# A DRAM-to-DRAM copy of x cut into 512 pieces of 5 KB instead of 64 of 40 KB, in a fused attention and feed-forward kernel

## The chip, the cores and the metric

The kernel runs on one core of one Trainium2 chip. The metric is the device time of one execution in microseconds (us). KB in the tables are units of 1024 bytes.

## The reference

One transformer block on 2048 tokens of width 640, with multi-query attention (32 query heads of 20 channels, one key and one value head) and a dense layer with squared ReLU, both on the same normalized input. Cut to what matters:

```python
xn = _layernorm(x, axis=-1)            # x: [1, 2048, 640] bf16
# attention: q = xn@wq as [32 heads, 2048, 20]; k = xn@wk, v = xn@wv are [2048, 20]
scores = einsum("bhqd,bkd->bhqk", q, k) * 20 ** -0.5
attn = (softmax(scores) @ v, heads joined) @ wo
# dense: h = relu(xn@w1 + b1) ** 2, 1536 wide
ffn = h @ w2 + b2
return x + attn + ffn
```

## The kernel before

**Attention.** The 2048 queries are four chunks of 512, the 32 heads eight groups of four; each of these 32 blocks runs over 16 tiles of 128 keys. For each key tile TensorE (PE) writes four 128x512 score tiles into PSUM (`q:` and `d:` in the written order). Their exponentials are taken either by ScalarE (ACT, L1083) or, by an integer approximation in four terms, by VectorE (DVE, L1093 and L1107), GpSimd (POOL, L1106) and accumulating DMAs (L1130). PE then multiplies the results with v (`v:` and `u:`).

**Fillers.** Between the score tiles PE does the projections and the dense layer: the transposes `T`, the keys `KT`, the values `V`, the queries `Q1` and `QC`, the dense layer `FFN`, `FP` and `OUT`.

**Order.** Each engine's instructions stand in a list written out by hand (`ORDER`, from L67), one list for PE, DVE, ACT, POOL and for the sync engine's queue of DMAs (SP). An engine works through its list in order and waits at an instruction until what it depends on is there. Every large load has a semaphore of its own.

**Start of SP's list:** `X0 X2 wq0 X4 X6 X8 b2 X12 xb b1 w11 wq w10 w20 w22 w23 w13 QD2_2 ...`. `X0` to `X12` (L622) load the rows of x into SBUF. `wq0` loads the first 80 columns of the query weights, `wq` (L628) the other 560 columns, as 128 partitions of 5 rows. `b1`, `w1`.. and `w2`.. are the bias and the weights of the dense layer. `HOLD` (L60) lets some of these wait for an evacuated transpose: `xb` and `wq` for `TE2`, `w11` for `TE6`, `w10` for `TE4`.

**The copy of x.** `xb` (L647) copies x from the input to a tensor in DRAM of the same shape. `XA` (L648) then adds the bias b2 to every row of that tensor, by an accumulating DMA issued from POOL that waits for `b2` (L646, 16 copies of b2 in DRAM) and for `xb`. Later `XR` (L869) loads the sum by 128 rows of tokens, sixteen times, as the residual that is added to the output.

**Around XA in POOL's list:** `... PW11 XN11 PW12 XA PW13 PW14 XN14 PW15 XN15 LIB p:27.1 ...`. `PW` (L676) makes the reciprocal standard deviation of 128 rows, `XN` (L677) normalizes them (rows 13 on DVE, 14 and 15 on POOL), and `T13` to `T15` on PE transpose the result. `LIB` loads another POOL library.

**Around Q1 in PE's list:** `q:38,39 q:40,41 Q1 Q1 T12 Q1 T13 q:42,43 Q1 q:44,45 Q1 KT6 ...`. `Q1` (L773) makes the queries of the second block in five steps and waits for `wq` and `wq0`.

**Four other copies of DRAM to DRAM** (`wd0` to `wd3`, L641 to L644) move rows of wo in about 100 to 150 us from the start: `wd0` 96 rows in one run of the outer dimension, the other three as 4 groups of 20, 12 and 8 rows, with the 4 outermost:

```python
wd8 = wod[96:128, 0, :].rearrange("(j r) n -> j r n", r=8)             # L638, j = 4
hrows = lambda r: A_wo[r:r + HPG * DH, :].rearrange("(j r) n -> j r n", r=DH)
```

Of the small transfers, `drs<-OR` (L945) moves 4 rows of 2 KB from SBUF, `R<-drs` (L946) 128 rows of 64 bytes, and `qT<-QCr` (L800) mostly 20 rows of 1 KB.

Of the kernel before, what the change touches and what calls it, by code (L numbers as in the profile page):

```python
# [38 lines left out]
def _pl(z):  # L39
# [20 lines left out]
HOLD = dict(wq="TE2", b1="TE5", w1=("TE4", "TE6", "TE8", "TE10"), w2=("TE12", "TE13", "TE14", "TE15"), wo=("RL3_2", "RL3_4"), wd="RL3_7",  # L60
            fr=[f"OUT{16 + k}.16" for k in range(4)])
# [433 lines left out]
def bass_parallel_sum__grouped_kv_mqa__dense_activation_squared_relu__prompt_kernel(nc, A_x, A_wq, A_wk, A_wv, A_wo, B_x, B_w1, B_b1, B_w2, B_b2, out):  # L495
    es = ExitStack()
    with es:
# [71 lines left out]
        xb = nc.dram_tensor("xb", [S, D], BF16, kind="Internal").ap()  # L569
# [14 lines left out]
        def one():  # L584
            nsem[0] += 1
            return newctr(f"d{nsem[0]}")
# [3 lines left out]
        def op(name, eng, fn, deps=(), **kw):  # L590
            o = Op(name, eng, fn if isinstance(fn, list) else [fn], deps, **kw)
            assert name not in made, name
            made[name] = o
            return o

        def load(name, eng, fn, deps=()):
            return op(name, eng, fn, deps, dma=one())
# [46 lines left out]
            lambda e: e.dma_start(wd32[:, DH:32, 1, :], hrows(wr0)[:, 8:DH, :])))]  # L644
        op("texp", "ACT", lambda e: e.preload_act_table_set("natural_log_exp_and_others"))
        l_b2 = load("b2", "SP", lambda e: e.dma_start(b2r[0].rearrange("(a n) -> a n", a=ST), B_b2.rearrange("(o n) -> o n", o=1).to_broadcast([ST, D])))  # L646
        l_xb = load("xb", "SP", lambda e: e.dma_start(xb.rearrange("(p a) d -> p (a d)", p=128), A_x[0].rearrange("(p a) d -> p (a d)", p=128)), [HOLD["wq"]])  # L647
        xa_op = op("XA", "POOL", lambda e: e.dma_start(xb.rearrange("(p a) d -> p (a d)", p=128).rearrange("p (k n) -> p k n", k=5),  # L648
                                                       b2r.rearrange("o (k n) -> o k n", k=5).to_broadcast([128, 5, 2048]), accum_op=ALU.add, max_dma_last_dim=4096), [l_b2, l_xb], dma=one())

# [379 lines left out]
        for e in ENG:  # L1030
            nth = {}
            for word in ORDER[e].split():
                w, _, ns = word.partition("@")
                ns = [int(x) for x in ns.split(",")] if ns else []
                k, _, a = w.partition(":")
# [64 lines left out]
        for u, x in sets.items():  # L1100
            assert sorted(x.order) == list(range(HPG))
            for j in range(1, NTERM):
                w = f"{u}.{j}"
                if ("p", w) in plan:
                    e, ns = plan["p", w]
# [3 lines left out]
                elif ("j", w) in plan:  # L1109
                    e, ns = plan["j", w]  # L1110
# [210 lines left out]
```

## Time and profile before

| | |
|---|---|
| median of 3 runs | 663.84 us (662.64 to 665.05) |
| profiled execution, its own time | 664.51 us |
| its span in the trace | 662.7 us |
| PE busy | 654.4 us, 99% of the span |
| ACT busy | 649.7 us, 98% |
| DVE busy | 625.3 us, 94% |
| POOL busy | 536.7 us, 81% |

The span is the stretch of the trace in which the engines work; the profiled execution's own time is 1.8 us longer. Times in the trace count from the start of the span. A line of a group names source line, engine, operation, output and inputs, count, busy time and the mean of one. "SPq" is the sync engine's queue, its durations are those of issuing a DMA and not of the transfer; how long a transfer took stands in the table of issues ("us to landing").

### The profile page before, as it was taken

The page shows a single profiled execution, that of the slowest core. Times are in us where ns is not written, and L with a number is a line of the kernel's source. Part 1 is how long each engine was busy: PE and PEld are TensorE (multiplying, and loading weights), DVE is VectorE, ACT ScalarE, POOL GpSimd, SP SyncE. Part 2 cuts the span into 40 slices and gives each one's busy share as a digit, 9 for nine tenths or more (in the row PEclk, how much of TensorE's full clock was granted, in tenths as well). Part 3 has the DMA queues.
Part 4 walks back from the last instruction along what each step waited for, and adds up shares of the span by engine and source line. Part 5 has one row for each costly group of instructions (what it writes and reads, how often), then busy time and mean ns, then how long its engine had stood idle before and what let it go on. Part 6 is the DMA issues. An engine that isn't in the chain of part 4 may idle for free.

```text
span 662.7 us, 22005 instructions
## 1 busy us (share of the span) xinstructions
PE 654.4 (99%) x9422; PEld 216.9 (33%) x9422; DVE 625.3 (94%) x1123; ACT 649.7 (98%) x716; POOL 536.7 (81%) x532
## 2 busy tenths in 40 slices
PE   8999999999999999999999999999999999999998
PEld 4432222333322223333332222333333322223444
DVE  8879999999999999999999999999999999999997
ACT  7999999999999999999999999999999999999996
POOL 1729899899898889898999989888999988899400
PEclk9999999999999999999999999999999999999999
DMA  8794857888897995696957645798888654858732
GB/s 293 187 245 96 185 110 163 166 183 187 185 186 161 183 182 120 129 184 125 178 107 155 122 92 99 151 189 170 158 174 165 132 121 91 178 105 177 141 110 71
DMA packets 53814, 102.06 MB, mean 154 GB/s; under 512 B 15948, under 2 KB 31452, under 8 KB 53652
## 3 DMA queue, kind: packets, MB, share of 16 engines
q0 software_dynamic: 18544, 68.17, 55.4%
q1 hardware_dynamic: 34308, 31.94, 16.8%
q8 instruction: 74, 1.21, 0.8%
q10 hardware_dynamic: 864, 0.54, 0.3%
q14 instruction: 24, 0.20, 0.1%
HBM read 23.26 MB, written 10.01 MB: 50 GB/s over the span
## 4 chain that ended last, share of the span: by engine, by line
PE 58%; ACT 34%; DMA 3%; DVE 3%; SPq 1%; issue 0%; POOL 0%
PE ps L600 57%; ACT PT L1083 34%; DVE tx L1093 1%; DMA tx<-tx 1%; DMA cmore<-drs 1%; DMA tx<-in_A_x_dram 1%; PE ps L1005 1%; SPq L800 0%; SPq L969 0%; SPq L963 0%; DVE xnT L694 0%; SPq L622 0%; DVE OR L662 0%; PE ps L700 0%; PE ps L703 0%
## 5 line engine op out<-in xcount | busy, mean ns | idle before, releaser
L1083 ACT ACTIVATE PT<-ps 128x1024 bf16<-128x1024 f32 (+1 forms) x693 | 640.4, 1089 | 2.3 <-PE ps L600 1.9
L1093 DVE TENSOR_SCALAR tx<-ps 128x512 uint16<-128x512 f32 x656 | 424.8, 683 | 21.8 <-PE ps L600 15.1
L1106 POOL INT64_ADD tx<-tx x375 | 396.3, 1132 | 54.3 <-DVE big L836 15.2
L600 PE MATMUL ps<-qT,kT 20*128 20x512 bf16 x2048 | 265.4, 384 | 3.3 <-ACT PT L1083 1.2
L600 PEld LDWEIGHTS ps<-qT,kT 20*128 20x128 bf16 x2048 | 69.0, 91 | 248.7 <-ACT PT L1083 132.4
L600 PE MATMUL ps<-PT,vx 128*32 128x512 bf16 x1392 | 131.7, 383 | 0.0
L1130 POOL DMA_DIRECT2D tx<-tx x118 | 121.3, 1028 | 10.3 <-POOL tx L1106 7.8
L600 PE MATMUL ps<-tx,vxs 128*32 128x512 bf16 x1220 | 115.4, 384 | 0.0
L600 PE MATMUL ps<-tx,vx 128*32 128x512 bf16 x864 | 81.3, 384 | 0.5 <-DMA tx<-tx 0.5
L600 PE MATMUL ps<-w_sb,big 128*32 128x320 bf16 x1536 | 79.1, 302 | 0.0
L600 PE MATMUL ps<-xnT,w_sb 128*32 128x512 bf16 x960 | 78.0, 383 | 0.0
L1107 DVE TENSOR_SCALAR tx<-tx 128x2048 uint16<-128x2048 uint16 x89 | 61.2, 700 | 0.6 <-PE ps L600 0.2
L600 PEld LDWEIGHTS ps<-PT,vx 128*32 128x32 bf16 x1392 | 34.6, 95 | 39.1 <-issue 31.1
L600 PEld LDWEIGHTS ps<-w_sb,big 128*32 128x32 bf16 x1536 | 33.8, 95 | 30.2 <-issue 20.0
L600 PEld LDWEIGHTS ps<-tx,vxs 128*32 128x32 bf16 x1220 | 30.0, 94 | 36.1 <-issue 27.1
L828 DVE TENSOR_SCALAR hT_tmp<-ps,b1col 128x512 bf16<-128x512 f32 x48 | 35.7, 744 | 0.8 <-PE ps L600 0.6
L600 PE MATMUL ps<-xnT,wq_sb 128*32 128x512 bf16 (+2 forms) x480 | 35.5, 357 | 0.0
L600 PEld LDWEIGHTS ps<-tx,vx 128*32 128x32 bf16 x864 | 21.4, 94 | 26.2 <-issue 21.5
L600 PEld LDWEIGHTS ps<-xnT,w_sb 128*32 128x32 bf16 x960 | 19.9, 95 | 28.8 <-issue 19.3
L600 PE MATMUL ps<-wo_c,OC 128*32 128x320 bf16 x496 | 28.0, 301 | 0.0
L1112 POOL INT64_ADD tx<-tx x14 | 26.9, 1924 | 0.9 <-DVE big L836 0.5
L944 DVE COPY OR<-ps 128x512 f32<-128x512 f32 x30 | 20.4, 680 | 1.7 <-PE ps L600 1.6
(87 smaller groups left out, 221.5 us busy)
## 6 DMA issues: line engine op xcount, KB each, us to landing
tx<-tx POOLq DMA_DIRECT2D x111, 512.0 KB, 5.9
tx<-tx POOLq DMA_DIRECT2D x7, 1024.0 KB, 8.8
w_sb<-in_B_w_dram SPq DMA_DIRECT2D x8, 480.0 KB, 9.6
big<-OR SPq DMA_DIRECT2D x71, 40.0 KB
xb<-in_A_x_dram SPq DMA_DIRECT2D x1, 2560.0 KB, 11.1
xb<-b2r POOLq DMA_DIRECT2D x1, 2560.0 KB, 19.8
xr<-xb SPq DMA_DIRECT2D x16, 160.0 KB, 3.2
out_dram<-out_sb SPq DMA_DIRECT2D x14, 160.0 KB, 3.6
```

The source lines that it names most:

```text
L600: return lambda e: e.matmul(out_(), l, val(r), start=val(start), stop=val(stop), tile_position=tp, skip_group_check=loose)
L828: o = evac(ref, f"RL{qc}_{f}", "DVE", lambda e: e.tensor_scalar(out=hT_tmp[:, k % 2, :], in0=ps[:, ref.n, :], scalar1=b1col[:, f:f + 1], s ...
L944: tn = evac(pv_ref[b], f"TN{b}", "DVE", lambda e: e.tensor_copy(out=OR[:, a, :], in_=acc()), or_users[a])
L1005: parts = [lambda e, l=l, r=r, first=first, last=last: e.matmul(ps[:, at(ref), 0:HW], l, r, start=first, stop=last, skip_group_check=k < N ...
L1083: o = op(f"a:{a}", e, lambda e, qk=qk, slots=slots: e.activation(out=some(PT, slots), in_=some(ps, [r.n for r in qk.takes]), func=AF.Exp, ...
L1093: o = op(f"e:{a}", e, lambda e, x=x, i=i, n=n, refs=refs: e.tensor_scalar(out=x.ref(0)[:, i * 512:(i + n) * 512].bitcast(U16) if n == 1 el ...
L1106: fn = dict(POOL=lambda e, x=x, j=j: e.int64_add(out=x.ref(j).bitcast(I64), in0=x.ref(0).bitcast(I64), in1=TSTEP * j * 0x0001000100010001) ...
L1107: DVE=lambda e, x=x, j=j: e.tensor_scalar(out=x.ref(j).bitcast(U16), in0=x.ref(0).bitcast(U16), scalar1=TSTEP * j, scalar2=None, op0=ALU.a ...
L1112: o = op(f"j:{w}", e, lambda e, x=x: e.int64_add(out=two(*sorted((x.at[2], x.at[3]))).bitcast(I64), in0=two(*sorted((x.at[0], x.at[1]))).b ...
L1130: fn = (lambda e, x=x: e.dma_start(*reversed(sums_of(x.at)), accum_op=ALU.add)) if k == "b" else (lambda e, x=x, p=pairs[0]: e.dma_start(x ...
```

## The change

The walk over x in the copy `xb` is written differently on both sides. Before, partition-like index p (128) was outermost and its 16 rows of 640 elements followed: all of it is one contiguous run, which went out as 64 pieces of 40 KB. After, each of the 128 stretches of 16 rows is cut into g = 4 parts of 4 rows (2560 elements, 5 KB), and g is put outermost: first the first parts of all 128 stretches, then the second parts, and so on. Same bytes, same places, same semaphore, same position in SP's list.

```diff
@@ -644,7 +644,7 @@
-        l_xb = load("xb", "SP", lambda e: e.dma_start(xb.rearrange("(p a) d -> p (a d)", p=128), A_x[0].rearrange("(p a) d -> p (a d)", p=128)), [HOLD["wq"]])
+        l_xb = load("xb", "SP", lambda e: e.dma_start(xb.rearrange("(p g a) d -> g p (a d)", p=128, g=4), A_x[0].rearrange("(p g a) d -> g p (a d)", p=128, g=4)), [HOLD["wq"]])
         xa_op = op("XA", "POOL", lambda e: e.dma_start(xb.rearrange("(p a) d -> p (a d)", p=128).rearrange("p (k n) -> p k n", k=5),
                                                        b2r.rearrange("o (k n) -> o k n", k=5).to_broadcast([128, 5, 2048]), accum_op=ALU.add, max_dma_last_dim=4096), [l_b2, l_xb], dma=one())
```

## The prediction

> **What bounds the kernel now.** I read the busy shares first, then the chain that ended last, then the first 60 us by engine, since the copy is issued at 9.8 us.
>
> ```profile
> PE 654.4 (99%) x9422; PEld 216.9 (33%) x9422; DVE 625.3 (94%) x1123; ACT 649.7 (98%) x716; POOL 536.7 (81%) x532
> PE 58%; ACT 34%; DMA 3%; DVE 3%; SPq 1%; issue 0%; POOL 0%
> ```
>
> The chain is PE for 58% and ACT for 34%: with both busy for 98 to 99% of the span, a stop of PE early on is never worked off. The copy itself is not in the chain. So the question is who waits for it, for what stands behind it in the queue, and with how much room. The timeline of the SP queue shows that neighbourhood (start, duration, line):
>
> ```profile
> 4.69 0.58 SPq L622 DMA_DIRECT2D tx<-in_A_x_dram  x1
> 9.80 0.50 SPq L647 DMA_DIRECT2D xb<-in_A_x_dram  x1
> 16.06 0.40 SPq L631 DMA_DIRECT2D b1row<-in_B_b_dram  x1
> 19.09 0.60 SPq L630 DMA_DIRECT2D w_sb<-in_B_w_dram  x1
> 19.73 0.64 SPq L628 DMA_DIRECT2D wq_sb<-in_A_wq_dram  x1
> 52.99 0.42 SPq L869 DMA_DIRECT2D xr<-xb  x1
> ```
>
> The table of issues gives their sizes and the us from issue to landing:
>
> ```profile
> xb<-in_A_x_dram SPq DMA_DIRECT2D x1, 2560.0 KB, 11.1
> xb<-b2r POOLq DMA_DIRECT2D x1, 2560.0 KB, 19.8
> wq_sb<-in_A_wq_dram SPq DMA_DIRECT2D x1, 700.0 KB, 5.7
> w_sb<-in_B_w_dram SPq DMA_DIRECT2D x8, 480.0 KB, 9.6
> b2r<-in_B_b_dram SPq DMA_DIRECT2D x1, 20.0 KB, 6.4
> wod<-in_A_wo_dram SPq DMA_DIRECT2D x1, 120.0 KB, 2.4
> wod<-in_A_wo_dram SPq DMA_DIRECT2D x1, 100.0 KB
> wod<-in_A_wo_dram SPq DMA_DIRECT2D x1, 60.0 KB
> wod<-in_A_wo_dram SPq DMA_DIRECT2D x1, 40.0 KB
> R<-drs SPq DMA_DIRECT2D x30, 8.0 KB, 4.1
> drs<-OR SPq DMA_DIRECT2D x30, 8.0 KB
> qT<-QCr SPq DMA_DIRECT2D x105, 20.0 KB
> ```
>
> The copy lands at 9.80 + 11.1 = 20.9 us, wq at 19.73 + 5.7 = 25.4. Who needs them, from the timelines of POOL, DVE and PE:
>
> ```profile
> 25.96 1.82 POOL L648 DMA_DIRECT2D xb<-b2r  x1
> 27.99 0.56 POOL L676 TENSOR_TENSOR rstd<-mv,nhalf 128x1 f32<-128x1 f32 x1 [0.21 <-DVE mv L667]
> 32.04 0.88 POOL L677 TENSOR_SCALAR big<-tx,mv,rstd 128x640 bf16<-128x640 bf16 x1
> 42.22 1.03 POOL L1106 INT64_ADD tx<-tx  x1 [9.31 <-DVE vxs L733]
> ...
> 29.00 0.75 DVE L677 TENSOR_SCALAR big<-tx,mv,rstd 128x640 bf16<-128x640 bf16 x2
> ...
> 29.29 0.61 PE L600 MATMUL ps<-xnT,wq_sb 128*20 128x512 bf16 x8
> 30.56 0.47 PE L700 MATMUL ps<-ident,big 128*128 128x128 bf16 x5
> 34.00 0.79 PE L700 MATMUL ps<-ident,big 128*128 128x128 bf16 x10
> 41.26 0.83 PE L600 MATMUL ps<-xnT,wq_sb 128*32 128x512 bf16 x12
> ```
>
> POOL reaches XA at 25.96, 5.0 us after the copy landed; PE reaches Q1 at 29.29, 3.9 us after wq landed. That is all the room there is.
>
> **The change: which engines carry it.** Sixteen DMA engines share a transfer. The profile prints a landing only where it finds sixteen increments for each issue. Beside the program, the rows above sort by the count of the outermost dimension: 64 (xb), 96 (wod, 120 KB), 128 (R, wq) and 16 (b2r) have a landing; 4 (the other three wod copies, drs<-OR) and 20 (qT) have none. So the outermost dimension is what is shared out, and one of 4 entries can occupy four engines at most. The new walk has g = 4 outermost on both sides: 2560 KB on four engines, 640 KB each, instead of 160 KB on sixteen. The size of a piece then matters little; the engines do. The three small wod copies are this very form, DRAM to DRAM.
>
> [...]
>
> **How long the copy takes.** DMA share and GB/s, the last two columns, while the copy runs on sixteen engines:
>
> ```profile
> 12.00:14.00 2.00, 1.57 (x41) 0.71 (x29) 2.00 (x10) 1.74 (x2) 1.13 (x2) 1.00 0.93 369
> 12.00:18.00 6.00, 5.08 (x94) 2.44 (x83) 5.45 (x22) 5.74 (x5) 3.11 (x5) 1.00 0.99 343
> 16.00:18.00 2.00, 1.75 (x35) 0.79 (x34) 1.71 (x7) 2.00 (x3) 0.91 (x2) 1.00 1.08 332
> ```
>
> A busy engine moves 369 / (16 x 0.93) = 24.8 GB/s at best, 343 / (16 x 0.99) = 21.7 over the six us, 332 / (16 x 1.08) = 19.2 at the end. I take 24.8: four engines ask DRAM for a quarter of that traffic, so the least disturbed row is the nearest. 655,360 B at 24.8 GB/s is 26.4 us (30.2 and 34.1 by the others). For what is fixed I take the 2.4 us of the 120 KB copy, which moves only 7.5 KB per engine. New landing: 9.80 + 2.4 + 26.4 = 38.6 us, 17.7 later.
>
> [...]
>
> **What that moves.** Issuing: 512 pieces instead of 64; the load at 4.69, also 512 pieces, took 0.58 against 0.50 us, and SP is free until 16.06. Nothing.
>
> POOL: XA waits from 25.96 to 38.6, and behind it in the list PW13, PW14, XN14, PW15, XN15 and LIB: +12.6. XN13 on DVE needs PW13: 38.6 + 2.0 (25.96 to 27.99) + 0.6 + about 0.5 = 41.7 instead of 29.75; T13 stood at 30.56. XN15 ended at 32.9, its transpose is in the group at 34.00: 1.1 us of room and more.
>
> SP's queue: it works in order; b2r, 20 KB issued behind the loads of x, took 6.4 us where 120 KB alone took 2.4. On the four engines b1, w11 (480 KB) and wq (700 KB) stand behind the copy; these last two spread over sixteen, so their share of 30 and 43.75 KB per engine comes after it: 1.2 + 1.8 us at 24.8 GB/s. wq lands at 38.6 + 3.0 = 41.6. PE stops at Q1 from 29.29 to 41.6: **+12.3 us**. T13, due at 30.56 + 12.3 = 42.9, finds XN13 done (41.7), so the two stops lie over each other and wq ends last. ACT has a few score tiles left and then stands too.
>
> Later users: b1 is needed just before 41.26, landed by 39; w10 lands 1.2 after wq. XA lands at 38.6 + 19.8 = 58.4, before the first XR (52.99 + 12.3 = 65.3). The first accumulation of POOL at 42.22 had waited 9.31 for DVE, so LIB fits. None adds.
>
> **The restart.** PE was busy nearly without a break from 29 us on, and would now pause for 12. Two rows show the same dummy matmul at the start and later:
>
> ```profile
> 2.57 4.60 PE L1041 MATMUL ps<-hT_tmp,OR 128*128 128x512 bf16 x13
> 12.44 0.59 PE L1041 MATMUL ps<-hT_tmp,OR 128*128 128x512 bf16 x2
> ...
> 30.00:40.00 10.00, 9.80 (x159) 4.50 (x157) 6.48 (x18) 9.93 (x12) 2.70 (x4) 1.00 1.05 210
> ```
>
> Two take 0.59 us, 0.21 apart and 0.38 for the last; thirteen at that pace are 2.9 us, at the start they took 4.60: 1.7 us lost, although the granted clock reads 1.00. No row shows a pause in the middle, so 0 to 1.7; I take 1.2, nearer to the start, which is the only row of a PE that had stood still. Against it stands that DVE, POOL and the loads catch up during the stop: at 30 to 40 us PE lacked 0.2 us, so I take off 0.3 (0 to 0.5).
>
> [...]
>
> **The sum.** 12.3 + 1.2 - 0.3 = +13.2 us. The profiled execution took 664.51 (span 662.7 and 1.8 around it), so it would be 677.7; it lies 0.7 over the median of 663.84, so the forecast for the median is 677.0, 2.0% slower. By bounds of the terms: 24.8 GB/s without restart and with 0.5 off, +11.8 (675.6); at 19.2 GB/s the copy is 7.7 longer and the two shares behind it take 3.9 instead of 3.0, so with 1.7 for the restart +22.6 (686.4).
>
> **The rivals.**
> - *Not slower: the copy stays on sixteen engines*, because the walk is put back into one run or shared out by the 128. It then lands near 21 us, before 25.96, and the time is 663.8. It decides at 13.8 us of transfer (25.96 - 9.80 - 2.4), which eight engines at 24.8 GB/s just reach (13.2). For it: the same bytes in the same places. Against: g stands outermost on both sides, with steps of 5 KB outside steps of 20 KB; only with the two loops exchanged would it be one run. 0.06.
> - *wq slips past the copy*, so that only XA's wait counts. T13 then moves from 30.56 to 41.7, +11.1, with the restart and what is caught up 675.8. Against: b2r's 6.4 us. 0.10.
> - *The four engines are slower*, as in the row 16 to 18, by traffic of their own: 680 to 686. The aggregate of 343 GB/s against 369 speaks for it, the quarter of the traffic against. 0.17.
> - *Fewer than four engines.* Two: 52.8 us, so 26.4 more, 703. 0.03.
> - *Faster*: smaller pieces let b1 and wq through sooner. wq already has 3.9 us of room, so it gives nothing unless it moves something I do not see. 0.01.
> - My forecast, 674 to 680: 0.63.
>
> **How the numbers follow.** About 0.3% (2 us) is what a measurement of this kernel can tell from no change. Slower: 0.63 + 0.10 + 0.17 + 0.03 = 0.93; same 0.06; faster 0.01. The range from 672.5 to 686 takes in the forecast, the second and most of the third rival, and at its lower end an engine faster than any row.
>
> **What the changed profile would show.** Landing of xb near 29 us instead of 11.1, or no landing at all in its row; XA on POOL at about 38.6; the first matmul of xnT and wq_sb with 512 columns at about 41.6, and behind it the DMA share near a quarter (0.25, some 100 GB/s) from 26 us on; from there everything moved by 12 to 14 us to the end. Wrong would be: XA still at 26, wq landing before the copy, or a stop that ACT and PE make up for by the end.

## The result, and the profile after

| | before | after |
|---|---|---|
| median of 5 runs each | 663.99 us (662.64 to 665.05) | 680.59 us (678.78 to 681.29) |
| ratio | | 1.0243, 95% interval 1.0221 to 1.0265 |
| profiled execution, its span | 664.51, 662.7 us | 679.16, 677.3 us |
| mean granted clock in the profiled execution | 1.000 | 0.987 |

The change costs 16.6 us. Medians, here and below, are over all executions of a kernel; ratios are formed from undisturbed ones only, which makes a visible difference in `e7_both` and `e9_both_16`.

The page of the changed kernel: busy shares, the chain's shares, the costliest group of ACT and three DMA issues (KB, us to landing).

```profile
PE 657.7 (97%) x9422; PEld 217.4 (32%) x9422; DVE 625.6 (92%) x1123; ACT 649.8 (96%) x716; POOL 536.7 (79%) x532
...
PE 61%; ACT 32%; DMA 4%; DVE 2%; POOL 0%; issue 0%
...
L1083 ACT ACTIVATE PT<-ps 128x1024 bf16<-128x1024 f32 (+1 forms) x693 | 640.6, 1089 | 16.7 <-PE ps L600 16.4
...
xb<-in_A_x_dram SPq DMA_DIRECT2D x1, 2560.0 KB
xb<-b2r POOLq DMA_DIRECT2D x1, 2560.0 KB, 19.2
...
wq_sb<-in_A_wq_dram SPq DMA_DIRECT2D x1, 700.0 KB, 18.4
```

The row of ACT's exponentials before:

```profile
L1083 ACT ACTIVATE PT<-ps 128x1024 bf16<-128x1024 f32 (+1 forms) x693 | 640.4, 1089 | 2.3 <-PE ps L600 1.9
```

The work is the same (the same counts, ACT busy for 649.8 us against 649.7). What has grown is idle time, for ACT's exponentials from 2.3 to 16.7 us, and PE's busy time: the same 9422 matmuls take 657.7 us instead of 654.4. The copy's row has lost its landing, as the four-group copies of wo have none, and wq takes 18.4 us to land instead of 5.7. The chain that ended last now has the copy in it. Its stretch around that (start, duration, engine):

```profile
9.80 27.90 DMA xb<-in_A_x_dram
37.70 0.31 issue
38.01 1.82 POOL xb L648
39.83 0.63 POOL rstd L676
...
40.48 0.45 DVE big L677
...
41.19 1.03 PE ps L600 x8
```

The copy takes 27.90 us and releases XA at 38.01; PW13 and XN13 follow, and PE goes on with Q1 at 41.19 (the chain puts Q1 down to XN13; the experiments will show that it waited for wq). The timeline of PE has the stop itself, the last entry of a line being the idle time before it:

```profile
28.94 0.40 PE L600 MATMUL ps<-qT,kT 20*128 20x512 bf16 x4
41.19 1.03 PE L600 MATMUL ps<-xnT,wq_sb 128*20 128x512 bf16 x8 [11.85 <-DVE mv L670]
```

The same first step of Q1 stood at 29.29 and took 0.61; now it takes 1.03. Why is in the windows (us; busy time of PE, PEld, DVE, ACT, POOL; then granted clock, DMA share, GB/s):

```profile
12.00:18.00 6.00, 5.49 (x106) 2.70 (x99) 5.60 (x24) 6.00 (x6) 3.10 (x5) 1.00 0.26 101
28.00:30.00 2.00, 1.34 (x31) 0.59 (x27) 1.37 (x5) 2.00 (x3) 0.00 (x0) 1.00 0.26 110
30.00:34.00 4.00, 0.00 (x0) 0.00 (x0) 0.00 (x0) 1.31 (x2) 0.00 (x0) 0.75 0.72 238
34.00:38.00 4.00, 0.00 (x0) 0.00 (x0) 0.00 (x0) 0.00 (x0) 0.00 (x0) 0.50 0.58 191
42.00:46.00 4.00, 4.00 (x30) 1.46 (x30) 1.10 (x4) 1.28 (x2) 2.02 (x3) 0.50 1.06 209
...
32.00:33.00 1.00, 0.00 (x0) 0.00 (x0) 0.00 (x0) 0.00 (x0) 0.00 (x0) 0.51 1.04 389
48.00:49.00 1.00, 1.00 (x12) 0.11 (x4) 0.00 (x0) 0.91 (x1) 0.00 (x0) 0.50 0.99 194
49.00:50.00 1.00, 1.00 (x18) 0.69 (x14) 0.26 (x1) 0.67 (x1) 0.00 (x0) 0.95 0.97 206
```

While the copy runs alone the DMA share is 0.26, four engines of sixteen. All compute engines stand at 34 to 38. The granted clock falls to half at 32.0 and is whole again only at 49.1, 7.9 us after PE had resumed and although PE shows as busy throughout.

How much the rest of the program has moved is read from one late instruction whose place in the lists is fixed, the second load of wo_c (L635; the two start times end the line). Before, then after:

```profile
L635 SPq DMA_DIRECT2D wo_c<-in_A_wo_dram x2: 434/439/444, 77.4 to 106.6; - x2
```

```profile
L635 SPq DMA_DIRECT2D wo_c<-in_A_wo_dram x2: 434/439/444, 92.5 to 121.8; - x2
```

106.6 has become 121.8: a **shift** of 15.2 us. ACT's score instructions, compared one by one, show the same 15.2 from 35 us (by the clock of before) on to 535, and the spans differ by 14.6 at the end. So 11.9 us are the stop, about 3.3 the restart, and only 0.6 is made up later.

### The profile page after: what moved, and what is told of

Same layout as the page of the kernel before. It is cut to its first block, busy times and chain, and to the rows that moved or that the text cites. A ratio compares the mean times of both kernels' runs of the same rounds, so it can differ in the third digit from the quotient of the medians.

```text
span 677.3 us, 22005 instructions
## 1 busy us (share of the span) xinstructions
PE 657.7 (97%) x9422; PEld 217.4 (32%) x9422; DVE 625.6 (92%) x1123; ACT 649.8 (96%) x716; POOL 536.7 (79%) x532
## 4 chain that ended last, share of the span: by engine, by line
PE 61%; ACT 32%; DMA 4%; DVE 2%; POOL 0%; issue 0%
PE ps L600 60%; ACT PT L1083 32%; DMA xb<-in_A_x_dram 4%; DVE tx L1093 1%; PE ps L1005 1%; POOL xb L648 0%; PE ps L700 0%; ACT xnT L696 0%; DVE OR L662 0%; DVE OR L663 0%; DVE ident L613 0%; DVE PT L611 0%; DVE big L677 0%; ACT OC L657 0%; POOL rstd L676 0%
## 5 line engine op out<-in xcount | busy, mean ns | idle before, releaser
L1083 ACT ACTIVATE PT<-ps 128x1024 bf16<-128x1024 f32 (+1 forms) x693 | 640.6, 1089 | 16.7 <-PE ps L600 16.4
L1093 DVE TENSOR_SCALAR tx<-ps 128x512 uint16<-128x512 f32 x656 | 425.0, 684 | 21.3 <-PE ps L600 14.6
L600 PE MATMUL ps<-tx,vxs 128*32 128x512 bf16 x1220 | 115.4, 384 | 0.0
L600 PE MATMUL ps<-xnT,wq_sb 128*32 128x512 bf16 (+2 forms) x480 | 36.5, 366 | 12.1 <-DVE mv L670 11.8
L600 PEld LDWEIGHTS ps<-w_sb,big 128*32 128x32 bf16 x1536 | 33.8, 95 | 30.2 <-issue 20.0
## 6 DMA issues: line engine op xcount, KB each, us to landing
w_sb<-in_B_w_dram SPq DMA_DIRECT2D x8, 480.0 KB, 10.4
```

The lines of the kernel that those rows point to most:

```text
L600: return lambda e: e.matmul(out_(), l, val(r), start=val(start), stop=val(stop), tile_position=tp, skip_group_check=loose)
L1083: o = op(f"a:{a}", e, lambda e, qk=qk, slots=slots: e.activation(out=some(PT, slots), in_=some(ps, [r.n for r in qk.takes]), func=AF.Exp, ...
L1093: o = op(f"e:{a}", e, lambda e, x=x, i=i, n=n, refs=refs: e.tensor_scalar(out=x.ref(0)[:, i * 512:(i + n) * 512].bitcast(U16) if n == 1 el ...
```

## The experiments

The theory: the copy runs on as many engines as its outermost dimension has entries, here four; XA and wq wait for it; PE stops, and restarts at half clock. The main rival at this point: the 512 smaller pieces themselves are slow. All edits are to the changed kernel unless said.

**Many small pieces on sixteen engines** (`e1_g16`).

```diff
-"(p g a) d -> g p (a d)", p=128, g=4
+"(p g a) d -> g p (a d)", p=32, g=16
```

> 512 pieces of 5 KB as in the change, in the same kind of order, but with g = 16 outermost instead of 4 (32 stretches of 64 rows, cut in 16). My theory (the four entries of the outermost dimension confine the copy to four engines): the copy lands near 21 us again, POOL reaches XA at 26.0 and PE reaches Q1 at 29.3 without waiting; time 664, within 2 us of the kernel before. Rival (the small pieces or the strided order make the copy slow): the copy lands near 38 and the time is 679 to 681.

Median 663.38 us, ratio 1.0004 (0.9982 to 1.0026). The copy lands after 12.2 us; from its window, POOL's and PE's timelines:

```profile
12.00:18.00 6.00, 5.42 (x109) 2.73 (x98) 5.67 (x24) 6.00 (x5) 3.11 (x5) 1.00 0.98 293
```

```profile
25.80 1.82 POOL L648 DMA_DIRECT2D xb<-b2r  x1
```

512 pieces of 5 KB, sixteen outermost: DMA share 0.98, XA does not wait, and the time is that of before. The copy lands 1.1 us later than before (12.2 against 11.1), within its 5.0 us of room; to the kernel the size of the pieces costs nothing here.

**Few large pieces on four engines** (`e2_g4_big`): `p=16, g=4` on both sides, 64 pieces of 40 KB as before the change, but g = 4 outermost.

> The other way round: 64 pieces of 40 KB as before, but with g = 4 outermost (16 stretches of 128 rows, cut in 4). My theory: four engines again, the copy lands near 37 to 39 us, time 679 to 682 as with the change. Rival (the size of the pieces): the copy lands near 21 and the time is 664.

Median 680.05 us, ratio 1.0247 (1.0230 to 1.0264): the whole loss, with the pieces of before.

```profile
12.00:18.00 6.00, 5.49 (x84) 2.79 (x75) 5.59 (x25) 6.00 (x6) 3.12 (x5) 1.00 0.21 86
```

```profile
40.98 1.04 PE L600 MATMUL ps<-xnT,wq_sb 128*20 128x512 bf16 x8 [12.17 <-DVE mv L670]
```

With the run above this decides between engines and pieces: the engines.

**Eight engines** (`e3_g8`): `p=64, g=8`.

> 512 pieces of 5 KB with g = 8 outermost. My theory: eight engines, 320 KB each; in the changed kernel an engine moved about 24.5 GB/s, so 13.4 us and some 2 fixed: landing at 25.0 to 25.6, just before POOL reaches XA (25.96); wq behind it lands about 3 us later, near 28, just before Q1 (29.29). Time 664 to 667. If a share of the engines does not count, only the pieces: 679 to 681. If the engine count counts but the loss is in proportion to the time of the copy (half of it): about 672.

Median 664.05 us, ratio 1.0016 (0.9999 to 1.0032). Window, POOL and PE:

```profile
12.00:18.00 6.00, 5.33 (x87) 2.58 (x76) 5.52 (x23) 5.87 (x5) 3.11 (x5) 1.00 0.52 199
```

```profile
27.19 1.82 POOL L648 DMA_DIRECT2D xb<-b2r  x1 [1.51 <-DMA xb<-in_A_x_dram]
```

```profile
30.21 0.61 PE L600 MATMUL ps<-xnT,wq_sb 128*20 128x512 bf16 x8 [1.14 <-DVE mv L667]
```

Half the engines are just short of enough: XA waits 1.51 us, PE 1.14, and the shift at wo_c is 1.0 (107.6). My expectation that the copy would land just ahead of XA failed by that much. The pause of 1.1 us leaves the clock whole. (The profiled execution took 668.53, 4.5 over its median. What it lost beyond the 1.0 lies behind a stop of 1.74 us at 170 us, after which the clock is at half from 174.0 to 180.9; the last section comes back to it.)

**Two engines** (`e8_g2`): `p=256, g=2`, 512 pieces of 5 KB.

> g = 2 outermost, 512 pieces of 5 KB. My theory: two engines, 1280 KB each at 24.4 GB/s, 53.7 us and 1.7 fixed: XA near 65, Q1 near 69 (w11 and wq still 3 us behind the copy), so a stop of about 39.5 us and 3 to 5 for the restart: 706 to 709. If the number of engines were four here too, 680.

One run, 705.13 us: DMA share 0.13 and 48 GB/s at 12 to 18 us, XA at 62.97, Q1 at 66.15 after a wait of 36.60; the time is just below the 706 to 709 expected. With two, four, eight and sixteen entries outermost the rows at 12 to 18 us read 48, 101, 199 and 293 GB/s at shares of 0.13, 0.26, 0.52 and 0.98. Sixteen times these shares is 2.1, 4.2, 8.3 and 15.7: about one busy engine for each entry.

**The restart by itself** (`e4_fill`): 52 groups of four matmuls on zeros ahead of Q1 keep PE busy while it would wait. Nothing else is changed.

```diff
-q:40,41@5,6 Q1@2 Q1 T12@1
+q:40,41@5,6 fill fill ... (52 times) Q1@2 Q1 T12@1
```

> The changed kernel with 52 additional groups of dummy matmuls on PE just ahead of Q1 (they add zero to an accumulator), about 11.2 us at full clock, so that PE does not stand still while it waits for wq. My theory (about 3.3 us of the loss come after the stop, because PE restarts at half clock): Q1 starts at 41.2 as with the change, the granted clock stays 1.0, the score tiles after 50 us are 11.9 to 12.3 us later than before instead of 15.2, and the time is 3 to 5 us below the changed kernel's, 676 to 677. Rival (the 3.3 us are ACT and DVE getting going again, or loads that land late): no gain, 679 to 681.

Median 674.76 us, ratio 1.0183 (1.0161 to 1.0206). PE's timeline and a window:

```profile
28.78 11.41 PE L600 MATMUL ps<-kT,zeros 128*32 128x512 bf16 x208
41.08 0.61 PE L600 MATMUL ps<-xnT,wq_sb 128*20 128x512 bf16 x8 [0.89 <-DVE mv L670]
```

```profile
42.00:46.00 4.00, 4.00 (x61) 1.76 (x60) 2.29 (x7) 2.81 (x4) 1.91 (x3) 1.00 1.05 206
```

Q1 starts at the same time (41.08), takes 0.61 again, the clock reads 1.00 (0.50 without the fill), and 61 matmuls run at 42 to 46 instead of 30. The shift is 11.8 (wo_c at 118.4): the wait and nothing more. So the restart costs 3.4 us at wo_c, 4.5 between the two spans (677.3 and 672.8) and 5.8 between the medians, more than the 3 to 5 us I expected. Adding useless work makes the changed kernel 0.9% faster.

**Each of the two waits alone.** XA and wq both wait for the copy; one move takes wq out of it (`e5_wq_first`), one takes XA off the way of XN13 (`e6_xa_late`).

```diff
-SP:   ... b2 X12 xb b1 w11 wq w10 ...
+SP:   ... b2 X12 wq xb b1 w11 w10 ...                        (e5)
-POOL: ... PW12 XA PW13 PW14 XN14 PW15 XN15 LIB ...
+POOL: ... PW12 PW13 PW14 XN14 PW15 XN15 XA LIB ...           (e6)
```

> The changed kernel with wq issued ahead of the copy in SP's list (wq xb b1 w11 w10 instead of xb b1 w11 wq w10). My theory (two waits lie over each other, wq on PE and the copy itself on POOL): Q1 now starts near 29.3, but T13 then waits for XN13, which waits for PW13 behind XA; the copy starts some 1.8 us later behind wq and lands near 39.5, T13 comes near 42.8 instead of 30.6. Time 679 to 682, no gain. Rival (wq behind the copy is the whole of it): 664 to 667.

> The changed kernel with XA moved behind XN15 in POOL's list (just ahead of LIB), so that no normalization stands behind the copy; wq stays behind it. My theory: POOL runs through to XN15 by 33, and PE still stops at Q1 until wq lands, 41.2. Time 678 to 681, no gain. Rival (POOL's wait for the copy at XA is the whole of it): 664 to 667.

`e5_wq_first`: 679.58 us, ratio 1.0209 (1.0157 to 1.0260). PE passes Q1 and stops soon after, at T13:

```profile
29.32 0.61 PE L600 MATMUL ps<-xnT,wq_sb 128*20 128x512 bf16 x8
...
42.96 0.73 PE L700 MATMUL ps<-ident,big 128*128 128x128 bf16 x5 [12.30 <-DVE mv L667]
```

`e6_xa_late`: 679.01 us, ratio 1.0199 (1.0148 to 1.0251). XA is issued at 45.51, XN13 is no longer late, and PE stops for wq:

```profile
41.67 1.04 PE L600 MATMUL ps<-xnT,wq_sb 128*20 128x512 bf16 x8 [11.30 <-DMA wq_sb<-in_A_wq_dram]
```

Neither move gains more than 1.6 us (0.2%): each wait is as long as the other and covers for it. They also correct a name. In the changed kernel the wait before Q1 is put down to a DVE instruction, but in `e5_wq_first`, with XA even later (39.99), the same Q1 runs at 29.32: what it waited for was wq, which landed at 22.70 + 18.4 = 41.1.

**Both moves** (`e7_both`), with `XR12` moved on in SP's list to stand ahead of `XR14`, so that SP does not wait for the later XA.

> Both moves together, and the first load of the sum (XR12) put just ahead of XR14 in SP's list, since XA now lands near 60. The copy still runs on four engines and lands near 39.5. My theory: with neither wq nor the normalizations behind it the 28 us are hidden; PE does not stop at 29 to 41. Left is LIB behind XA on POOL, at about 41.5 instead of 33: if the library loads fast, 664 to 665, if it takes the 9 us that POOL had to spare, its first addition comes up to 8 us late and the time is up to 669. Rival (four engines loaded for 28 us disturb the kernel in another way, by bandwidth or by full queues): 672 or more.

679.48 us, ratio 1.0139 (1.0041 to 1.0236), its executions from 671.46 to 686.99. My expectation of 664 to 669 failed. The stop at 29 to 41 us is gone, but a new one has come:

```profile
62.83 0.61 PE L600 MATMUL ps<-qT,kT 20*128 20x512 bf16 x4 [4.05 <-DMA qT<-QCr]
```

XA, now at 39.92, fills the engines for some 20 us (DMA share 0.94 to 1.09 from 38 to 58 us) exactly when the queries of the next blocks are being moved. The clock is at half from 60.4 to 84.3 us. Not all of this execution's loss lies there: by 21 us it was already 3.6 us behind, after a stop of only 1.31 us. PE's timeline and two windows:

```profile
15.05 0.61 PE L600 MATMUL ps<-qT,kT 20*128 20x512 bf16 x6 [1.31 <-DVE mv L664]
```

```profile
12.00:18.00 6.00, 4.56 (x80) 2.28 (x77) 4.62 (x20) 4.86 (x5) 2.23 (x4) 0.84 0.50 185
18.00:24.00 6.00, 6.00 (x73) 2.59 (x71) 4.32 (x16) 4.31 (x5) 2.84 (x4) 0.59 0.26 109
```

Two runs took this apart: the same lists with the copy on sixteen engines (`e9_both_16`, `p=32, g=16`), and the four-engine copy with XA still later, behind `j:31.2` in POOL's list (`e10_later`).

> The same three moves in the lists as in e7_both (wq ahead of xb, XA behind XN15, XR12 next to XR14), but with the copy on sixteen engines (p=32, g=16). If what e7_both still lost comes from XA being late (39.92 us) and meeting the loads of QC's queries, then here, where XA should be issued near 33.5 us (after XN15), XA is out of the way by about 54 us, the stop at 58 to 62 us is gone or small, and the time is 663 to 667. If instead it comes from the moves in the lists themselves (XA beside the loads at 40 to 58 us at all, or xb later on behind wq), the stop stays and the time is 672 or more.

> The copy of the changed kernel on four engines, wq ahead of xb, XR12 next to XR14 as in e7_both, and XA moved on in POOL's list to behind the first five steps of VectorE's and POOL's exponentials (behind j:31.2, near 53 us), where the loads of QC's queries are through and XA waits for no copy. If the meeting of XA with those loads was e7_both's new stop, PE has no stop over 1 us between 28 and 62 us and the shift at 62 us is under 2 us, and the time is 664 to 669; XA's transfer now lies beside the first accumulating DMAs of the exponentials (60 to 74 us), which can give 1 to 4 us back. If any late XA costs the same, the time stays at 676 to 682, with a wait for a DMA of tx or qT between 60 and 80 us.

`e9_both_16`: median 668.83 us, ratio 1.0052 (1.0017 to 1.0087). XA is at 32.94, and PE still stops, for half as long:

```profile
56.63 0.40 PE L600 MATMUL ps<-qT,kT 20*128 20x512 bf16 x4 [1.93 <-DMA qT<-QCr]
```

The shift is 2.0 (wo_c at 108.6), the clock 1.000. `e10_later`: median 673.27 us, ratio 1.0118 (1.0068 to 1.0169), XA at 53.23 without a wait. No stop at 29 to 62 us, but then:

```profile
74.35 0.62 PE L600 MATMUL ps<-tx,vxs 128*32 128x512 bf16 x4 [5.00 <-DMA tx<-tx]
```

Its shift is 8.8 (115.4): 5.0 of wait, and half clock from 73.4 to 80.3. Both of my ranges missed, by 1.8 and 4.3 us (663 to 667, 664 to 669). The first's condition held only in part, so each explanation seems to have a share: of e7's stop of 4.05 us, 1.93 remains with the copy on time, and comes from the moves; the rest goes with XA's lateness. That rests on one trace of each, and e7's had the early loss besides. The second's mechanism was as expected (a wait for `tx`) and dearer than the 1 to 4 us I gave it. Wherever XA's 20 us of all engines were put after 33 us, PE then waited for another DMA: 1.9 us from 33, 4.1 from 40, 1.2 from 45.5 (`e6_xa_late`, for qT at 69.76) and 5.0 from 53. From 26 us, where it stood, there was no such wait. Between `e7_both` and `e10_later` only XA's place differs, and the wait moved from `qT` to `tx`; that XA's transfer causes all four is argued from this, since no run leaves it out. The best version found with the four-engine copy is thus `e10_later`, 7.3 us better than the changed kernel and 9.8 worse than before; none beats before.

## Why the prediction was right, point by point

- **Four engines at most: right.** That all four would be used, which the sum takes for granted, was my assumption; the profile before did not print it. The runs show it: DMA share 0.26, that is 4.2 of sixteen engines. The landings recorded in the trace say the same: sixteen for the copy before, five after, one at 10.9 us, just behind the issue, and four at 37.1 to 37.7. And `e1_g16`, `e2_g4_big`, `e3_g8` and `e8_g2` leave nothing to the size of the pieces.
- **24.8 GB/s per engine and 2.4 us fixed: right in the sum.** The copy was through 27.9 us after its issue, 37.7 instead of 38.6. The window at 12 to 18 gives 101 / (16 x 0.26) = 24.3 GB/s. The slower rows at 16 to 18 us, the third rival's reason, did not apply. Nor need sixteen engines be that slow: in `e9_both_16` they moved 389 GB/s at a share of 1.04 at 12 to 18, 23.4 each. The two parts were less exact than their sum: at 24.3 GB/s the bytes take 27.0 us, which leaves some 0.9 and not 2.4 for what is fixed. The faster engine that the lower end of the range allowed for rested on no row.
- **XA at 38.6, wq at 41.6: right within 0.6 us** (38.01 and 41.1), and with them the stop: 11.85 us measured against 12.3. "The two stops lie over each other and wq ends last" is what `e5` and `e6` show; taking away either leaves the other.
- **wq slips past the copy** (the second rival): no. It landed 3.4 us behind it. But the queue did more than the prediction said; see the last section.
- **Eight engines decide: nearly.** `e3_g8` waits 1.51 us at XA. The prediction had it just reach the point (13.2 us against 13.8); it just misses it.
- **The restart, +1.2 us with bounds of 0 and 1.7: the mis-sized term.** It measured 3.3 to 3.4 us in the traces, twice the upper bound, and 5.8 us between the medians of `e4_fill` and the changed kernel. The ruler was too short: I took the loss from the dummy matmuls at the program's start and noted a granted clock of 1.00 there. But in the trace of before the record of the clock begins only at 5.85 us; up to 5.5 us these matmuls start 0.43 us apart, from 5.9 on 0.21, so they too ran at half speed, for some 4 us. The real restart ran at a granted clock of 0.50 for 7.9 us, in which PE shows as busy throughout; the clock had fallen at 32.0 us, 2.7 us after the stop began.
- **Caught up, -0.3: about right.** The shift of 15.2 is 14.6 at the end.
- **The sum.** 12.3 + 1.2 - 0.3 = 13.2 against a span longer by 14.6: the restart's error of +2.1, less 0.4 in the stop and 0.3 in what was caught up. The medians differ by 16.6, and 2.0 of that lies between the profiled execution and the others, which no trace shows. Mean granted clocks of 0.982 to 0.987 in those executions (0.987 in the profiled one, from 17.1 us at half clock) suggest longer stretches at half clock, some 24 us for 0.982 by an estimate from these figures; that is argued, not shown.
- **The band: missed.** 680.59 lies above the 674 to 680 that I gave 0.63, and in the 680 to 686 of the third rival, whose mechanism, slower engines, did not occur. The path was mine, and the size of the restart was not.

## What to carry to other kernels

In this copy it was the outermost dimension that was shared out over the DMA engines: 2, 4, 8 and 16 entries on both sides gave shares of 0.13, 0.26, 0.52 and 0.98. Of the transfers in the prediction's list those with a multiple of sixteen entries outermost have a landing, those with 4 or 20 have none. So look at that count before the size of the pieces (5 or 40 KB made no difference to the kernel's time here: 663.38 and 663.99 us on sixteen engines, 680.59 and 680.05 on four). When a transfer becomes late, count everything behind it: who waits for it, what stands after it on its engines, and where it and its followers will now run; taking away one of two equal waits gains nothing, and a large transfer that is moved, as XA was, takes its 20 us of all engines with it. In five traces a stop of PE of 11 to 37 us cost its length and a restart of 1.7 to 4.9 us, which PE multiplying zeros saved in `e4_fill`. Shorter stops differed: some of 1.1, 1.3 and 1.9 us left the clock whole, others of 1.3 and 1.7 us were followed by 6.8 us at half clock.

## What was not expected of the hardware

**The clock comes back late, and in steps.** In seven traces with a stop of over 4 us the stretch at half clock, read from windows of 1 us, lasted 13.7 (`e6`), 17.1 (after), 20.5 (`e2`), 20.5 (`e5`), 44.4 (`e8`), 6.8 (`e10`) and 23.9 us (`e7`). Four of these lengths lie 3.4 us apart (13.7, 17.1, 20.5, 23.9), and 6.8 and 44.4 are 2 and 13 times as much; a step of about 3.4 us is thus an estimate from these lengths. Two more stretches, both of 6.8 us, followed stops that were shorter by far: of 1.31 us in `e7_both` (half clock from 16.1 to 22.9) and of 1.74 us in `e3_g8` (174.0 to 180.9). Stops of 1.14 us (`e3_g8`), 1.32 us (`e6_xa_late`, at 10.7 us) and 1.93 us (`e9_both_16`) left the clock whole, so the length of a stop alone does not decide. What else does was not tested.

After PE had resumed from a long stop, the clock stayed at half for 3.9 us in `e6`, 7.9 in the changed kernel, 10.0 in `e8`, 10.4 in `e5` and 12.6 in `e2`; the shift that came with the stop, less its wait, was 1.7, 3.4, 3.9, 4.0 and 4.9 us, some 0.4 us for each us at half clock. So one term varies from kernel to kernel with the same stop. What brings the clock back, no run tells: the records show PE as busy for all of these times.

**Issuing took longer behind a copy on few engines.** SP's timeline in the changed kernel (durations are those of issuing):

```profile
9.80 0.74 SPq L647 DMA_DIRECT2D xb<-in_A_x_dram  x1
16.07 5.92 SPq L631 DMA_DIRECT2D b1row<-in_B_b_dram  x1
22.04 0.62 SPq L630 DMA_DIRECT2D w_sb<-in_B_w_dram  x1
22.70 7.00 SPq L628 DMA_DIRECT2D wq_sb<-in_A_wq_dram  x1
29.74 5.31 SPq L630 DMA_DIRECT2D w_sb<-in_B_w_dram  x1
```

Issuing b1, 0.40 us before, took 5.92; wq 7.00 instead of 0.64. With two engines b1 took 30.69. That the four engines' queues were full is my inference from this, shown by no view. What the trace shows is that wq was late not only behind the copy but in being issued, and the part of it on the other twelve engines was late as well: twelve of its sixteen landings stand at 33.4 to 33.8 us and four at 40.4 to 41.0, where before all sixteen stood at 24.6 to 25.5. It cost nothing more here, as `e2_g4_big` shows: with 16 pieces for each engine instead of 128, b1 took 0.36 us to issue and wq left at 19.21, yet wq landed 21.6 us later, at 40.8, against 41.1.

```profile
19.21 0.64 SPq L628 DMA_DIRECT2D wq_sb<-in_A_wq_dram  x1
19.90 14.89 SPq L630 DMA_DIRECT2D w_sb<-in_B_w_dram  x1
```
